# Attention's pooled v taken from a TensorE product of 32-row blocks, with its own loads and GpSimd sums left out, and the merge moved to the head of an iteration

## The chip, the cores and the metric

One core of a Trainium2 chip runs the whole program. The metric is device time in microseconds (us) for one execution; lower is better. Engines are named as in the profile: PE is TensorE (PEld its weight loads), DVE is VectorE, ACT is ScalarE, POOL is GpSimd, SP is the engine that here issues almost all DMAs.

## The reference, cut to what matters

```python
# q, k, v: (4, 8, 576, 64) fp32; factor = 4, Sd = 144
q_d, k_d, v_d = (t.reshape(B, H, Sd, factor, D).mean(axis=3) for t in (q, k, v))
out_up = np.repeat(sm_attn(q_d, k_d, v_d), factor, axis=2)      # pooled attention, 144 x 144
mask = np.abs(pos[:, None] - pos[None, :]) < factor
attn = softmax(np.where(mask, scale * q @ k^T, -1e9))           # local attention, a band of 7
x = (out_up + attn @ v) -> (2304, 512)
x = moe(x)      # two dense layers, 512 -> 2048 -> 512, mish between them
out = moe2(x)   # 8 experts, one chosen per token, 512 -> 1024 -> 512
```

## The kernel before

The program runs in three parts: attention, the dense layers (`moe1`) and the experts (`moe2`). The change touches attention alone.

**Units and iterations.** Attention works on 16 units, one for each batch b (4) and pair of heads (4 in a batch). A loop over `it` = 0..19 (line 561) runs them as a software pipeline, with every engine's instructions in the order in which the code is written: iteration `it` transposes and copies q and k of unit it+1 (`transposes`, L381 to L383 on PE; `copies` and `p_copies`, L392 to L405 on ACT), makes the scores of unit it (`scores`, L413 and L418; `p_scores`, L453), normalizes unit it-1 (`normalize`, L434 to L437; `p_normalize`, L469 to L471), makes the outputs of unit it-2 (`outputs`, L499 for the pooled part, L504 for the local part) and adds both parts up for unit it-3 (`merge`, L518 on DVE, and a store to `x_t` by SP, L533). After the outputs come the softmaxes of unit it (L426 to L428, L462, L464), and `scatter` (L443, L360, L447), `p_transposes` (L479) and `pt_copies` (L486) of unit it-1.

**v stands twice in SBUF.** The local part multiplies by 32-row blocks of v: `load_v(b, n)` issues six DMAs (L340), each with 32 rows of all 8 heads, 64 KB in pieces of 256 bytes; 24 of them fill one of the two tiles `vw` for a batch. One quarter n of a batch is loaded at the end of each iteration. A block starts 4 rows ahead of the 24 rows of queries that it serves, so that 8 rows of each block stand in a neighbour too. The pooled part has loads of its own: `load_v4(j, c)` fetches 288 rows of four heads (288 KB, in pieces of 1 KB, L330), and `pool_v(j, c)` sums groups of four rows in two additions on POOL (L354, L355), once in each iteration, behind `pool_qk` (L347, L348) on the same engine.

**Weights.** `prep_step` spreads the splitting of the dense layers' weights over the iterations (lines L199 to L219 on ACT and DVE, loads L184 and L186 on SP). From iteration 5 on there is some in each iteration.

**PSUM.** Eight banks go around: `bank()` gives the next one at each call, ten calls in an iteration, and whoever writes first into a bank waits for the last reader of its former content. The two banks of the local outputs are read last by `merge`, one iteration later.

**Queues.** All loads and stores of this stage go through SP in the order of the code, so a load that waits for its buffer holds everything written behind it.

Of the kernel before, what the change touches and what calls it, by code (L numbers as in the profile page):

```python
# [23 lines left out]
def moe_kernel(ctx: ExitStack, tc: tile.TileContext, q, k, v, w_in, w_out, modality, w_gate, w_gate_t, m_bias, w1, w2, out):  # L24
# [133 lines left out]
    LAG = 5  # L158
    LA = 1
    SC_A = (0, 1)  # L160
# [80 lines left out]
    NP = H // 2  # L241
# [5 lines left out]
    SPL = S // 4  # L247
    HS = SPL // 2
    CT = S // 128
# [4 lines left out]
    def attention(acx, xcx, tcx):  # L254
# [19 lines left out]
        pbd = [spare[2 + i][:, :2 * S].rearrange("p (t h i q) -> p t h i q", t=T, h=2, i=4) for i in range(2)]  # L274
        vw = [ac.tile([128, T, H * D], F32, name=f"vw{i}") for i in range(2)]
        x0 = ac.tile([128, NP, BT], F32, name="x0")

        def setup_a():
# [26 lines left out]
        def setup_p():  # L305
            for t in pbd:
                G.memset(t, 0.0)
# [18 lines left out]

        def load_v4(j, c):
            b, h0 = j // 2, j % 2 * HB
            v4 = ld.tile([HS, HB, 4, D], F32, tag="v4", name="v4")
            SP.dma_start(out=v4.rearrange("p h r d -> p h (r d)"), in_=v[b, h0:h0 + HB, c * 4 * HS:(c + 1) * 4 * HS, :].rearrange("h (p r) d -> p h (r d)", r=4))  # L330
            bt[j]["v4", c] = v4

        def load_v(b, n):
# [16 lines left out]

        def pool_v(j, c):
            v4 = bt[j]["v4", c]
            vp = wk.tile([HS, HB, D], F32, tag="vp", name="vp", bufs=6)
            G.tensor_tensor(v4[:, :, 0:2], v4[:, :, 0:2], v4[:, :, 2:4], op=ALU.add)  # L354
            G.tensor_tensor(vp, v4[:, :, 0], v4[:, :, 1], op=ALU.add)  # L355
            bt[j]["vp", c] = vp

# [98 lines left out]
        def p_softmax(u):  # L456
            psc = st.pop(("ps", u))
            pe = wk.tile([128, LQ, SPL], F32, tag="pe", name="pe")
            pm = wk.tile([128, LQ], F32, tag="pm", name="pm")
            pz = wk.tile([128, LQ], F32, tag="pz", name="pz")  # L460
            p3 = psc[:, :LQ * SPL].rearrange("p (g s) -> p g s", g=LQ)
            V.tensor_reduce(pm, p3, axis=X, op=ALU.max, negate=True)  # L462
            for g in range(LQ):
                A.activation(pe[:, g], p3[:, g], AF.Exp, bias=pm[:, g:g + 1], accum_out=pz[:, g:g + 1])  # L464
            st["p", u] = (pe, pz)

        def p_normalize(u):
            pe, pz = st["p", u]
            V.tensor_scalar(pz, pz, 1e-9, 4.0, op0=ALU.add, op1=ALU.mult)  # L469
            V.reciprocal(pz, pz)  # L470
            G.tensor_tensor(pe, pe, pz.unsqueeze(2).to_broadcast([128, LQ, SPL]), op=ALU.mult)  # L471

        def p_transposes(u):
            pe, _ = st.pop(("p", u))
            tps = [bank(f"tp{c}") for c in range(2)]
            for c in range(2):
                for g in range(LQ):
                    n = min(128, 2 * SPL - 128 * g)
                    PE.transpose(tps[c][:HS, 128 * g:128 * g + n], pe[:n, g, HS * c:HS * c + HS], ident[:n, :n])  # L479
            st["q", u] = tps  # L480

        def pt_copies(u):
            tps = st[("q", u)]
            pp = wk.tile([HS, 2, 2 * SPL], F32, tag="pp", name="pp", bufs=1)
            for c in range(2):
                A.copy(pp[:, c], tps[c][:HS, :2 * SPL])  # L486
            st["q", u] = pp

        def outputs(u):
            j, p = divmod(u, NP // 2)  # L490
            b, pg = divmod(u, NP)
            vp, w_ = [bt[j]["vp", c] for c in range(2)], vw[b % 2]
            pp = st.pop(("q", u))
# [3 lines left out]
            for c in range(2):  # L497
                for h in range(2):
                    PE.matmul(po[64 * h:64 * h + 64], vp[c][:, 2 * p + h], pp[:, c, SPL * h:SPL * h + SPL], start=c == 0, stop=c == 1, tile_position=(0, 64 * h))  # L499
            o = [bank(f"xo{i}") for i in range(2)]  # L500
# [46 lines left out]
        load_a(1)  # L547
        for c in range(2):
            load_v4(0, c)
        for n in range(NP - 1):  # L550
            load_v(0, n)
            if n == LA:
                load_a(2)
        setup_p()
        for z in range(2):
            pool_qk(1, z, V if z else G)
        pool_v(0, 0)
        load_v4(1, 0)
        copies(0)
        p_copies(0)  # L560
        for it in range(U + 4):
            if it == U - 1:
# [4 lines left out]
                split_x(0, *range(KD))  # L567
            new, mid, old = it < U, 0 < it <= U, 2 <= it < U + 2
            if it + 1 < U:
                transposes(it + 1)  # L570
                copies(it + 1)
                p_copies(it + 1)
            if mid:
                normalize(it - 1)
                p_normalize(it - 1)
            if 3 <= it < U + 3:
                merge(it - 3)
            if new:
# [632 lines left out]
```

## Time and profile before

| what | us |
|---|---|
| median of 3 runs (843.55 to 846.75) | 845.87 |
| the profiled execution's own time | 849.41 |
| its span, first to last instruction | 847.7 |
| PE, DVE, ACT, POOL busy in the span | 761.4, 593.6, 526.9, 220.3 |

The page gives busy time of each engine, a picture of the span in 40 slices (about 21.2 us each), the chain of waits that ended last, and groups of instructions by line. Attention takes about the first eight slices. A row of the timeline has the start, the duration, the engine, the source line, the operation with what it writes and reads, the count, and in square brackets how long the engine sat idle before and who released it. SPq stands for the issue of a DMA by SP's queue. The mean granted TensorE clock over the span is 0.954 of full speed.

### The profile page before, as it was taken

What the parts mean: (1) busy time and instruction counts of PE and PEld (TensorE: products, weight loads), DVE (VectorE), ACT (ScalarE), POOL (GpSimd) and SP (SyncE); (2) the same over time, 40 slices, a digit from 0 to 9 for tenths busy, and PEclk for the clock granted to TensorE, in tenths of its full rate; (3) what the DMA queues carried; (4) which work ended last, traced back from release to release, by engine and by line L of the source; (5) the groups of instructions that cost most, each with busy time, mean ns of one, the idle gap of its engine ahead of it and who ended that gap; (6) DMA issues with size and microseconds to landing.
All of it is one profiled execution on the core that took longest, in us unless ns stands there. A gap on an engine that the chain in (4) does not pass through costs nothing. (4 is left out here: it accounts for less than half of the span.)

```text
span 847.7 us, 14454 instructions
## 1 busy us (share of the span) xinstructions
PE 761.4 (90%) x5078; PEld 644.4 (76%) x5078; DVE 593.6 (70%) x1414; ACT 526.9 (62%) x1019; POOL 220.3 (26%) x212
## 2 busy tenths in 40 slices
PE   5597786799979999999999899899789999999991
PEld 4475665588858888888899788789688887899981
DVE  6499998689966874388439658968766555666652
ACT  6597886899846556655666567554336554565551
POOL 7577673100000000000000110337323232332330
PEclk9699988999979999999999999999999999999996
DMA  7999991455623110010001004546577667767762
GB/s 171 221 185 217 233 239 62 142 149 180 192 66 127 63 26 0 14 57 20 0 13 58 20 29 183 76 39 197 103 223 222 208 194 235 223 228 240 199 213 63
DMA packets 90066, 112.99 MB, mean 133 GB/s; under 512 B 39915, under 2 KB 62077, under 8 KB 89725
## 3 DMA queue, kind: packets, MB, share of 16 engines
q1 hardware_dynamic: 85421, 101.35, 44.7%
q0 software_dynamic: 4560, 10.60, 3.6%
q8 instruction: 42, 0.69, 0.4%
q14 instruction: 43, 0.35, 0.2%
HBM read 97.06 MB, written 15.12 MB: 132 GB/s over the span
## 5 line engine op out<-in xcount | busy, mean ns | idle before, releaser
L731 DVE TENSOR_TENSOR t<-bk,t 128x512 f32<-128x512 f32 (+1 forms) x80 | 50.0, 633 | 100.8 <-ACT t L725 100.8
L678 POOL DMA_INDIRECT ids_by_expert<-tok_id,g_pi x18 | 20.8, 1154 | 279.1 <-DVE run L677 104.3
L638 DVE SCALAR_TENSOR_TENSOR junk<-o,wgb 128x512 f32<-128x512 f32 x120 | 85.0, 708 | 2.9
L719 ACT ACTIVATE t<-bk 128x512 f32<-128x512 f32 (+1 forms) x80 | 44.0, 550 | 54.5 <-PE bk L711 52.8
L740 DVE TENSOR_TENSOR gg<-t,gg 128x512 fp32r<-128x512 f32 (+1 forms) x80 | 57.3, 720 | 7.5 <-ACT gg L729 4.2
L729 ACT CAST gg<-t 128x512 fp32r<-128x512 f32 (+1 forms) x57 | 32.7, 573 | 40.0 <-DVE t L731 33.7
L711 PE MATMUL bk<-x,wi0h 128*128 128x512 f32 (+1 forms) x160 | 52.3, 407 | 5.4 <-DVE x L699 5.1
L720 ACT ACTIVATE t<-t,half 128x512 f32<-128x512 f32 (+1 forms) x80 | 54.6, 682 | 2.6
L1097 POOL DMA_INDIRECT out_dram<-yo,oid x19 | 25.4, 1338 | 115.7 <-ACT yo L1096 69.2
L1083 ACT ACTIVATE hT<-bk 128x256 fp32r<-128x256 f32 x80 | 30.4, 383 | 35.6 <-PE bk L1081 33.1
L725 ACT ACTIVATE t<-t,hpi 128x512 f32<-128x512 f32 (+1 forms) x80 | 52.2, 674 | 0.2
L711 PE MATMUL bk<-x,wi1h 128*128 128x512 f32 (+1 forms) x160 | 47.8, 381 | 4.2 <-DVE t L731 4.2
L751 PE MATMUL bk<-wo1h,gg 128*128 128x512 f32 x144 | 48.3, 406 | 0.0
L1084 DVE SCALAR_TENSOR_TENSOR hT<-bk,hT 128x256 fp32r<-128x256 f32 x80 | 32.9, 420 | 21.5 <-ACT hT L1083 21.4
L711 PE MATMUL bk<-x,wi3h 128*128 128x512 f32 (+1 forms) x160 | 46.9, 375 | 0.6 <-DVE rank L673 0.6
L711 PE MATMUL bk<-x,wi2h 128*128 128x512 f32 (+1 forms) x160 | 46.1, 369 | 0.0
L751 PE MATMUL bk<-wo3h,gg 128*128 128x512 f32 x144 | 46.1, 392 | 0.0
L751 PE MATMUL bk<-wo0h,gg 128*128 128x512 f32 x144 | 45.9, 393 | 0.0
L751 PE MATMUL bk<-wo2h,gg 128*128 128x512 f32 x144 | 45.8, 392 | 0.0
L711 PEld LDWEIGHTS bk<-x,wi0h 128*128 128x128 f32 x160 | 31.9, 204 | 13.6 <-DVE x L699 7.0
L711 PEld LDWEIGHTS bk<-x,wi1h 128*128 128x128 f32 x160 | 30.6, 195 | 8.9 <-DVE t L731 4.6
L1081 PE MATMUL bk<-x,ew10h 128*128 128x256 f32 x160 | 31.8, 288 | 5.7 <-DVE x L1016 2.4
(308 smaller groups left out, 2338.2 us busy)
## 6 DMA issues: line engine op xcount, KB each, us to landing
est<-in_moe_w_dram SPq DMA_DIRECT2D x88, 512.0 KB
wst<-in_moe_w_in_dram SPq DMA_DIRECT2D x16, 512.0 KB
wst<-in_moe_w_out_dram SPq DMA_DIRECT2D x16, 512.0 KB
vw<-in_v_dram SPq DMA_DIRECT2D x88, 64.0 KB
v<-in_v_dram SPq DMA_DIRECT2D x16, 288.0 KB
x_second<-o SPq DMA_DIRECT2D x18, 256.0 KB
kn<-in_k_dram SPq DMA_DIRECT2D x8, 512.0 KB
qn<-in_q_dram SPq DMA_DIRECT2D x8, 512.0 KB
```

Source lines behind the costliest of these rows:

```text
L638: V.scalar_tensor_tensor(wgb["junk"], x2[tl], 1.0, wgb[e], op0=ALU.mult, op1=ALU.mult, accum_out=gate[tl][:, e:e + 1])
L711: PE.matmul(h, a[:, f % QF, kk], x[:, c], start=n == 0, stop=n == 3 * KD - 1)
L719: A.activation(t, bk[f % GF][:, :BLK[j]], AF.Tanh, scale=0.5)
L720: A.activation(t, t, AF.Arctan, scale=-0.5, bias=half)
L725: A.activation(t, t, AF.Sin, scale=-2.0, bias=hpi)
L729: A.copy(gg[:, 0], t_)
L731: V.tensor_tensor(t, bk[f % GF][:, :BLK[j]], t, op=ALU.mult)
L740: V.tensor_tensor(gg[:, 1], t, gg[:, 0], op=ALU.subtract)
L751: PE.matmul(acc[t], gg[:, a, c], w[:, f % QF], start=f == 0 and n == 0, stop=f == NF - 1 and n == 2)
L1081: PE.matmul(ps[:, :256], W1(i, a, kk, f), xt[i][:, c, kk], start=n == 0, stop=n == 3 * KD - 1)
L1083: A.activation(hT[:, 0, f], ps[:, :256], AF.Relu)
L1084: V.scalar_tensor_tensor(hT[:, 1, f], ps[:, :256], 0.0, hT[:, 0, f], op0=ALU.max, op1=ALU.subtract)
```

## The change

- `load_v4` and `pool_v` go, with their 16 loads and 32 POOL additions.
- A constant `pool_v` tile (128 x 32) is made once: column a has ones on the four rows of each block that form pooled row a, 6 columns for each of the 24-row stretches, and zeros in the last 8 columns.
- `pool_vw(b)`, once in a batch at the end of iteration 4b+1, multiplies `pool_v` by the six 512-column tiles of `vw`: six fp32 matmuls into 32-partition strips of two banks, then two copies on ACT into `vp`. Pooled rows so stand at 24 of every 32 partitions, and the pooled probabilities `pe` are laid out the same way: they go to two fixed tiles that POOL clears once, ACT's exponentials and POOL's normalization write 24 of every 32 columns, and `p_transposes`, `pt_copies` and the pooled products work on 128 and 64 rows where they worked on 72 and 72.
- The blocks of batch 0 are all loaded ahead of the loop, before `load_a(2)`; those of batch b+1 at iterations 4b+1 (two quarters), 4b+2 and 4b+3, not one quarter at 4b+1 to 4b+4.
- `merge(it - 3)` stands at the head of an iteration, ahead of the transposes and of `normalize`.

```diff
+        pool_v = ac.tile([128, W], F32, name="pool_v")
+        pes = [ac.tile([128, LQ, T, W], F32, name=f"pe{i}") for i in range(2)]
...
-        def load_v4(j, c):
...
-        def pool_v(j, c):
-            v4 = bt[j]["v4", c]
-            vp = wk.tile([HS, HB, D], F32, tag="vp", name="vp", bufs=6)
-            G.tensor_tensor(v4[:, :, 0:2], v4[:, :, 0:2], v4[:, :, 2:4], op=ALU.add)
-            G.tensor_tensor(vp, v4[:, :, 0], v4[:, :, 1], op=ALU.add)
-            bt[j]["vp", c] = vp
+        def pool_vw(b):
+
+            ps = [bank(f"pv{c}") for c in range(2)]
+            for t in range(T):
+                c, i = divmod(t, 4)
+                PE.matmul(ps[c][32 * i:32 * i + 32], pool_v, vw[b % 2][:, t], tile_position=(0, 32 * i))
+            vp = wk.tile([128, 2, H * D], F32, tag="vp", name="vp", bufs=1)
+            for c in range(2):
+                A.copy(vp[:KP[c], c], ps[c][:KP[c]])
+            st["v"] = vp
...
-                A.activation(pe[:, g], p3[:, g], AF.Exp, bias=pm[:, g:g + 1], accum_out=pz[:, g:g + 1])
+                A.activation(pe[:, g, :, :QB], p3[:, g].rearrange("p (t a) -> p t a", t=T), AF.Exp, bias=pm[:, g:g + 1], accum_out=pz[:, g:g + 1])
...
-        for c in range(2):
-            load_v4(0, c)
-        for n in range(NP - 1):
+        for n in range(NP):
             load_v(0, n)
-            if n == LA:
-                load_a(2)
+        load_a(2)
...
+            if 3 <= it < U + 3:
+                merge(it - 3)
             if it + 1 < U:
                 transposes(it + 1)
...
-            if 3 <= it < U + 3:
-                merge(it - 3)
...
-            m, odd = divmod(it + 1, 2)
-            b, n = divmod(it + NP - 1, NP)
-            if b < B:
-                load_v(b, n)
-            if m < NH:
-                pool_v(m, odd)
-            if m + 1 < NH:
-                load_v4(m + 1, odd)
+            b, n = divmod(it, NP)
+            if n == 1 and b < B:
+                pool_vw(b)
+            if n and b + 1 < B:
+                for z in ((), (0, 1), (2,), (3,))[n]:
+                    load_v(b + 1, z)
```

Line numbers of the changed kernel are 5 or 6 higher in the functions below `pool_vw`: L479 becomes L485, L381 becomes L386, L518 becomes L524.

The first place is PE at the end of iteration 1. The rows are PE's instructions from the pooled scores of unit 1 to the first transposes of unit 3; `bk` is a PSUM bank, `rl` the relaid k or q. Before:

```order
L453 MATMUL bk_95<-kp,qbd_168 128x144 x3
L479 MATMUL bk_96<-ident,pe 72x128 x2
L479 MATMUL bk_96<-ident,pe 72x32
L479 MATMUL bk_97<-ident,pe 72x128 x2
L479 MATMUL bk_97<-ident,pe 72x32
L381 MATMUL bk_90<-ident,rl 128x128 x4
L382 MATMUL bk_92<-ident,pl 128x128
```

and now:

```order
L458 MATMUL bk_95<-kp,qbd_168 128x144 x3
L485 MATMUL bk_96<-ident,pe_172 128x128 x2
L485 MATMUL bk_96<-ident,pe_172 128x32
L485 MATMUL bk_97<-ident,pe_172 64x128 x2
L485 MATMUL bk_97<-ident,pe_172 64x32
L357 MATMUL bk_90<-vw_169,pool_v 32x512 x4
L357 MATMUL bk_91<-vw_169,pool_v 32x512 x2
L386 MATMUL bk_92<-ident,rl 128x128 x4
L387 MATMUL bk_94<-ident,pl 128x128
```

Six products with 512 columns that read all of `vw` now stand ahead of the transposes of unit 3, and the banks that follow are two further on.

The second place is SP's queue from the loads ahead of the loop to the end of iteration 1 or 2. Before:

```order
L330 DMA v_267<-in_v_dram 72x4x256
L330 DMA v_269<-in_v_dram 72x4x256
L340 DMA vw_169<-in_v_dram 28x8x64
L340 DMA vw_169<-in_v_dram 32x8x64 x11
L323 DMA kn<-in_k_dram 128x4x256
L324 DMA rm<-in_k_dram 64x4x64
L323 DMA qn<-in_q_dram 128x4x256
L324 DMA rm<-in_q_dram 64x4x64
L340 DMA vw_169<-in_v_dram 32x8x64 x6
L330 DMA v_309<-in_v_dram 72x4x256
L184 DMA wst<-in_moe_w_in_dram 128x4x128
L340 DMA vw_169<-in_v_dram 32x8x64 x5
```

and now:

```order
L341 DMA vw_169<-in_v_dram 28x8x64
L341 DMA vw_169<-in_v_dram 32x8x64 x22
L341 DMA vw_169<-in_v_dram 28x8x64
L330 DMA kn<-in_k_dram 128x4x256
L331 DMA rm<-in_k_dram 64x4x64
L330 DMA qn<-in_q_dram 128x4x256
L331 DMA rm<-in_q_dram 64x4x64
L183 DMA wst<-in_moe_w_in_dram 128x4x128
```

All 24 blocks of batch 0 stand in one run ahead of the third pair of k and q loads; before, that pair and a weight load stood between them.

The third place is DVE from the scatter of one unit to the next softmax, in an iteration of batch 1 where no weights are split. Before:

```order
L443 STREAM_TRANSPOSE et<-e 128x384
L360 TENSOR_REDUCE spare_101<-et 32x12x24 x2
L434 TENSOR_REDUCE sm<-e 128x12
L435 TENSOR_SCALAR sm<-sm 128x12
L436 RECIPROCAL sm<-sm 128x12
L469 TENSOR_SCALAR pz<-pz 128x3
L470 RECIPROCAL pz<-pz 128x3
L518 TENSOR_TENSOR x_171<-bk_92,pos 128x288
L518 TENSOR_TENSOR x_171<-bk_93,pos 128x224
L518 TENSOR_TENSOR x<-bk_93,pos 128x64
L360 TENSOR_REDUCE rl<-qn 128x512
```

and now:

```order
L448 STREAM_TRANSPOSE et<-e 128x384
L365 TENSOR_REDUCE spare_101<-et 32x12x24 x2
L524 TENSOR_TENSOR x_174<-bk_94,pos 128x288
L524 TENSOR_TENSOR x_174<-bk_95,pos 128x224
L524 TENSOR_TENSOR x<-bk_95,pos 128x64
L439 TENSOR_REDUCE sm<-e 128x12
L440 TENSOR_SCALAR sm<-sm 128x12
L441 RECIPROCAL sm<-sm 128x12
L474 TENSOR_SCALAR pz<-pz 128x3
L475 RECIPROCAL pz<-pz 128x3
L365 TENSOR_REDUCE rl<-qn 128x512
```

The three additions of the merge stand ahead of the normalization; nothing else on DVE has moved there.

## Rows read from the trace of the kernel before

**Rows 1.** Busy time by stretch; columns: us, then busy us of each engine
```profile
core 0: us, PE busy (x) PEld busy (x) DVE busy (x) ACT busy (x) POOL busy (x), PEclk, DMA share, GB/s
24.00:41.40 17.40, 9.26 (x108) 6.79 (x106) 7.82 (x22) 8.83 (x27) 10.46 (x12) 0.65 1.12 230
41.40:60.80 19.40, 18.86 (x316) 15.16 (x315) 16.45 (x39) 18.63 (x65) 13.93 (x15) 0.97 0.88 176
60.80:134.00 73.20, 60.45 (x935) 47.34 (x934) 70.07 (x138) 61.58 (x198) 51.98 (x52) 0.91 0.95 221
...
250.00:600.00 350.00, 340.67 (x1659) 290.75 (x1658) 237.98 (x682) 207.38 (x325) 52.30 (x34) 0.99 0.24 63
```
**Rows 2.** Timeline of PE and POOL, 24 to 42 us
```profile
24.07 0.33 PE L413 MATMUL bk<-mask,id_b 128*128 128x384 bf16 x1
...
31.07 0.59 PE L504 MATMUL bk<-spare,vw 128*64 128x96 f32 x4 [3.79 <-DMA vw<-in_v_dram]
31.92 1.26 POOL L354 TENSOR_TENSOR v<-v 72x512 f32<-72x512 f32 x1 [4.53 <-DMA v<-in_v_dram]
...
36.60 0.59 PE L504 MATMUL bk<-spare,vw 128*64 128x96 f32 x4 [0.93 <-DMA vw<-in_v_dram]
...
41.37 0.53 PE L413 MATMUL bk<-mask,id_b 128*128 128x384 bf16 x1
```
**Rows 3.** Timeline of SP's DMA issues, 0 to 40 us
```profile
6.61 1.88 SPq L330 DMA_DIRECT2D v<-in_v_dram  x2
8.60 12.19 SPq L340 DMA_DIRECT2D vw<-in_v_dram  x12
20.89 0.40 SPq L323 DMA_DIRECT2D kn<-in_k_dram  x1
...
23.35 3.06 SPq L340 DMA_DIRECT2D vw<-in_v_dram  x6
...
28.46 3.86 SPq L340 DMA_DIRECT2D vw<-in_v_dram  x6
```
**Rows 4.** Timeline around iteration 6, 63 to 71 us
```profile
63.20 0.35 SPq L533 DMA_DIRECT2D x_t<-x  x1
...
66.43 0.43 PE L504 MATMUL bk<-spare,vw 128*64 128x96 f32 x4 [2.05 <-DMA vw<-in_v_dram]
...
68.83 0.82 DVE L518 TENSOR_TENSOR x<-bk,pos 128x288 f32<-128x288 f32 x2 [1.11 <-DMA x_t<-x]
```
**Rows 5.** Groups of DVE instructions by line, 60.8 to 134 us; count, busy us, mean ns
```profile
L204 DVE TENSOR_SCALAR wm<-wm 128x512 int32<-128x512 int32 x5 | 8.8, 1754 | 0.0
...
L214 DVE SCALAR_TENSOR_TENSOR wm<-wst,wm 128x512 int32<-128x512 int32 x5 | 5.7, 1135 | 0.0
...
L219 DVE TENSOR_TENSOR wi0l<-wm,wi0h 128x512 fp32r<-128x512 f32 x3 | 4.1, 1360 | 0.0
L209 DVE SCALAR_TENSOR_TENSOR wm<-wst,wm 128x512 int32<-128x512 int32 x4 | 4.1, 1016 | 0.0
L469 DVE TENSOR_SCALAR pz<-pz 128x3 f32<-128x3 f32 x9 | 3.2, 355 | 0.0
```
**Rows 6.** The same lines by source, whole span: ns least/median/most
```profile
L204 DVE TENSOR_SCALAR wm<-wm x32: 417/428/3674, 70.2 to 236.4; 128x512 int32<-128x512 int32 x32
L469 DVE TENSOR_SCALAR pz<-pz x16: 103/105/1412, 18.9 to 149.6; 128x3 f32<-128x3 f32 x16
L209 DVE SCALAR_TENSOR_TENSOR wm<-wst,wm x32: 681/692/1762, 88.8 to 243.1; 128x512 int32<-128x512 int32 x32
```
**Rows 7.** Groups of POOL instructions by line, 60.8 to 134 us
```profile
L354 POOL TENSOR_TENSOR v<-v 72x512 f32<-72x512 f32 x10 | 13.6, 1358 | 9.3 <-DMA v<-in_v_dram 9.1
...
L355 POOL TENSOR_TENSOR vp<-v 72x256 f32<-72x256 f32 x10 | 7.3, 731 | 0.8
```
**Rows 8.** Timeline of PE, 76 to 84 us: tiled fp32 matmuls
```profile
78.00 0.88 PE L418 MATMUL bk<-spare,qT 128*32 128x64 f32 x48
81.73 1.16 PE L504 MATMUL bk<-spare,vw 128*64 128x96 f32 x24
```
**Rows 9.** Groups by line, 0 to 170 us: a full-width ACT copy; POOL memset
```profile
L394 ACT COPY qT<-bk 128x512 f32<-128x512 f32 x16 | 9.4, 587 | 0.2
...
L307 POOL MEMSET spare<- 128x1152 f32 x2 | 2.3, 1166 | 0.1
```
**Rows 10.** Timeline around iteration 15, 138 to 145 us
```profile
141.96 0.23 DVE L436 RECIPROCAL sm<-sm 128x12 f32<-128x12 f32 x1
142.33 0.81 DVE L518 TENSOR_TENSOR x<-bk,pos 128x288 f32<-128x288 f32 x2
...
142.84 1.23 PE L504 MATMUL bk<-spare,vw 128*64 128x96 f32 x12 [4.83 <-DVE x L518]
```

More of the change, by code (lines that the diff above doesn't have):

```diff
@@ L158, in moe_kernel @@
     LAG = 5
-    LA = 1
     SC_A = (0, 1)
@@ L247, in moe_kernel @@
     SPL = S // 4
-    HS = SPL // 2
+    KP = (128, 32 * (T - 4))
     CT = S // 128
@@ L285, in setup_a @@
             V.tensor_copy(pool_id[:, :, RP:], ident[:2 * CR, :2 * CR].rearrange("p (z r) -> p z r", z=2))
+            V.memset(pool_v, 0.0)
+            V.tensor_reduce(
+                pool_v[:, :QB].rearrange("p (i a) -> p i a", i=4),
+                ident.rearrange("p (i w) -> p i w", i=4)[:, :, 4:4 + QB].rearrange("p i (a f) -> p i a f", f=4),
+                axis=X, op=ALU.add,
+            )
             V.tensor_copy(id_b, ident)
@@ L305, in setup_p @@
         def setup_p():
-            for t in pbd:
+            for t in pbd + pes:
                 G.memset(t, 0.0)
@@ L325, in load_a @@
             bt[j] = {"n": (kn, qn), "rm": rm}
-        def load_v4(j, c):
[L328 to L331, printed above, removed]
         def load_v(b, n):
@@ L457, in p_softmax @@
             psc = st.pop(("ps", u))
-            pe = wk.tile([128, LQ, SPL], F32, tag="pe", name="pe")
+            pe = pes[u % 2]
             pm = wk.tile([128, LQ], F32, tag="pm", name="pm")
@@ L470, in p_normalize @@
             V.reciprocal(pz, pz)
-            G.tensor_tensor(pe, pe, pz.unsqueeze(2).to_broadcast([128, LQ, SPL]), op=ALU.mult)
+            p4 = pe[:, :, :, :QB]
+            G.tensor_tensor(p4, p4, pz.unsqueeze(2).unsqueeze(3).to_broadcast([128, LQ, T, QB]), op=ALU.mult)
         def p_transposes(u):
@@ L478, in p_transposes @@
                     n = min(128, 2 * SPL - 128 * g)
-                    PE.transpose(tps[c][:HS, 128 * g:128 * g + n], pe[:n, g, HS * c:HS * c + HS], ident[:n, :n])
+                    PE.transpose(tps[c][:KP[c], 128 * g:128 * g + n], pe[:n, g, 4 * c:min(4 * c + 4, T)].rearrange("p t a -> p (t a)"), ident[:n, :n])
             st["q", u] = tps
@@ L483, in pt_copies @@
             tps = st[("q", u)]
-            pp = wk.tile([HS, 2, 2 * SPL], F32, tag="pp", name="pp", bufs=1)
+            pp = wk.tile([128, 2, 2 * SPL], F32, tag="pp", name="pp", bufs=1)
             for c in range(2):
-                A.copy(pp[:, c], tps[c][:HS, :2 * SPL])
+                A.copy(pp[:KP[c], c], tps[c][:KP[c], :2 * SPL])
             st["q", u] = pp
@@ L491, in outputs @@
             b, pg = divmod(u, NP)
-            vp, w_ = [bt[j]["vp", c] for c in range(2)], vw[b % 2]
+            vp, w_ = st["v"], vw[b % 2]
             pp = st.pop(("q", u))
@@ L498, in outputs @@
                 for h in range(2):
-                    PE.matmul(po[64 * h:64 * h + 64], vp[c][:, 2 * p + h], pp[:, c, SPL * h:SPL * h + SPL], start=c == 0, stop=c == 1, tile_position=(0, 64 * h))
+                    PE.matmul(po[64 * h:64 * h + 64], vp[:KP[c], c, (2 * pg + h) * D:(2 * pg + h + 1) * D], pp[:KP[c], c, SPL * h:SPL * h + SPL], start=c == 0, stop=c == 1, tile_position=(0, 64 * h))
             o = [bank(f"xo{i}") for i in range(2)]
@@ L556, in attention @@
             pool_qk(1, z, V if z else G)
-        pool_v(0, 0)
-        load_v4(1, 0)
         copies(0)
```

## The prediction

> **What bounds the kernel now.** I read the busy time by stretch first, with the starts of iterations as bounds, then the timeline in the stretch that looked worst, then the groups by line where an engine was full. The reader is to see four stages in [rows 1]. From 24 to 41 us nothing is full: one iteration takes 17.3 us, the TensorE clock is 0.65, and the DMA engines are the busy ones. From 41 to 61 us iterations take about 6.5 us, and ACT (18.63 of 19.40) and PE (18.86) are full. From 61 to 134 us nine iterations take 8.1 us each, and DVE is full (70.07 of 73.20). Behind attention PE is full (340.67 of 350.00 in the long middle); nothing there changes, so what attention gains or loses shifts the end by as much.
>
> The slow iteration has its reason in the timeline: the local outputs of unit 0 wait for blocks of v, 3.79 us in the first of three such waits, and end at 37.2; POOL sits 4.53 us for v rows meanwhile [rows 2]. SP shows why: the first 12 blocks took 12.19 us to issue, the third k and q load stands before the next six, and the last six go out at 28.46 to 32.3 [rows 3]. The same wait, shorter, comes in iteration 6 (2.05 us), where DVE also waits 1.11 us for an earlier store [rows 4].
>
> In the DVE stage the full engine isn't only at work. L204 takes 417 ns at best and up to 3674; five of them here mean 1754 [rows 5, 6]. Whenever I looked, POOL was inside an addition at that time. Above their least times (L214 and L219 have about L209's least time, 0.68 us) the groups of [rows 5] carry: L204 5 x 1.34 = 6.7, L214 5 x 0.455 = 2.3, L219 3 x 0.68 = 2.0, L209 4 x 0.335 = 1.3, L469 9 x 0.252 = 2.3 us; 14.6 us together, a fifth of the stage.
>
> **The change part by part.**
>
> *The start: -4.0 us.* The wait for batch 0's blocks moves from the outputs in iteration 2 to the pooled product at the end of iteration 1, where PE's queue is held with the transposes of unit 3 behind it. When are 24 blocks there? SP is free for them at about 8.5 us. The first eight I leave at the old pace of 1.02 us (they came behind two v loads that are gone, so this is slow enough: 16 us); the other 16 at 0.51 to 0.64 us (3.06 and 3.86 for six, [rows 3]) make 24 to 26 us, landing some 2 us later. With about 1 us for the last pair of products PE goes on at 27 to 29 us. Then come the transposes, scores and outputs of iteration 2, 6 to 8 us by the clock, so that iteration 3's transposes start at 33 to 37 us, where they started at 38.65, behind the last wait of [rows 2]. The middle is a gain near 4 us. Bounds: -7 (blocks at 0.51 us from the first) and +4 (all 24 at 1.02 us: 33 us, and outputs at about 41). The k and q loads of unit pair 2 are issued 3 to 5 us later than at 20.89; they are first needed in iteration 2, which starts later too.
>
> *Iteration 6: -1.5 us.* Batch 1's last blocks are issued an iteration earlier, so the 2.05 us wait goes; DVE's next limit is close (its own 1.11 us, [rows 4]), so I take 1.5, between 0 and 2.
>
> *POOL's additions: -5.0 us.* In the DVE stage they are 13.6 + 7.3 = 20.9 of POOL's 51.98 us [rows 1, 7], 40%. In proportion, 14.6 x 0.40 = 5.9 us of DVE's excess go. I take 5.0, because the merge no longer stands between the normalization and the weight splitting, which so falls nearer to the start of POOL's remaining run of additions. Bounds: nothing (the rest of POOL's work meets DVE as before) and 9.3 us (if the excess falls as the square of what is left, 0.6). In other stages ACT, PE or DMA set the pace, and I count nothing there.
>
> *The pooled products: +2.1 us.* No row has an fp32 product with 512 columns in strips of 32. The nearest: 24 products of 64 columns, four strips wide, take 0.88 us, so 6 streams of 64 columns, 2.3 ns a column; 12 products of 96 columns, two wide, take 1.16, so 2.0 ns a column [rows 8]. A batch has a stream of four and one of two, 1024 columns: 2.1 to 2.4 us side by side; one after the other, six times 512 columns at 2.0 ns, 6.2 us. I take 2.1. The Trainium skill ("TensorE: Matmul & The Clock Gate", "Why this matters for your kernels") has three strips of 32 with 512 columns gain 2.38 times, not 3; by that I would estimate 2.6 us and the sum would be 0.5 us higher; the four-wide row stands between. Iteration 1 has its product inside the first term. Iteration 5 lies where PE and ACT are full, so it pays in full; the two copies on ACT, 2 x 0.587 us [rows 9], run while PE does the next transposes. Iterations 9 and 13 lie in the DVE stage, where PE and ACT have some 12 us to spare in nine iterations [rows 1]: nothing. If DVE's excess fell so far that PE became the bound, they would cost up to 2 us each.
>
> *The merge ahead of the normalization: -1.0 us.* DVE does as much as before. At iteration 15 the second half of the outputs waits 4.83 us for the merge, which stands behind normalization steps from 141.16 to 142.33 us [rows 10]; it comes 1.2 us earlier. I take 1.0; bounds 0 and 1.2. The normalization itself starts 0.81 us later, covered by POOL, which waits for DVE in every iteration.
>
> *SP's new order: +1.0 us.* At iterations 5 and 9, twelve blocks (6 to 10 us by [rows 3]) stand ahead of a store of `x_t`. The tile that the store reads has two buffers, and DVE's merge two iterations on waits for it; the 1.11 us of [rows 4] is that wait, for a store issued 5.6 us earlier. Iterations of 6.5 to 8 us leave 13 to 16 us for load, blocks, store and landing, so it just fits; I take one more wait like the one seen.
>
> *Small ones: +0.8 us.* Transposes and pooled products on 128 rows where there were 72 load wider weights: 0.5 over 16 units (nothing where PE has room). One memset and one reduction more on DVE ahead of the loop: 0.3. Two clears of 128 x 576 on POOL, 0.6 us each by half of L307 [rows 9], take the place of two sums there. The exponentials, copies and normalization have as many elements as before: nothing. The 16 loads taken out lighten DMA queues that are 0.88 to 1.12 busy [rows 1]; what that gives is in the terms above.
>
> Sum: -4.0 - 1.5 - 5.0 + 2.1 - 1.0 + 1.0 + 0.8 = **-7.6 us**. It is made against the profiled execution, 849.41 us, and gives 841.8 there. That execution lies 3.5 us above the median of the runs, 845.87; I carry the difference over: **838.3 us**.
>
> **The rivals.**
>
> *PE held at the start, no gain there (843 us).* A queue that works in order stands still until the last block lands. The old stall dropped the clock to a mean of 0.65 [rows 1]; a new stall of 5 us in iteration 1 can do the same, and iteration 2 then runs at 1.2 GHz. The Trainium skill (same page, same section) warns that an idle gap between bursts of matmuls brings the half clock back; the trace agrees with its 0.65. The first term becomes 0 to +1: 845.9 - 3.1 = 842.8. For it: 12 blocks did take 12.19 us. Against: six took 3.06, with no k or q load between.
>
> *DVE stays slow (843 us).* The excess is made by POOL's remaining 31 us as before, since those run right behind the normalization, where the weight splitting falls. The third term is 0: 843.3. For it: L204's wait is longer than any one addition. Against: the additions removed stand right ahead of L469 of the next iteration, and it is in the list.
>
> *More than forecast (830 us).* DMA is the hidden bound: with 4.7 MB less, blocks land at the fast pace (-7), the merge's wait goes (-1 instead of +1) and DVE's excess falls by 9. That is -7.6 - 3 - 2 - 3 = -15.6, so 830.3. For it: a DMA share near 1 for 120 us. Against: in the DVE stage no engine but POOL waits long for a load.
>
> *Stores behind the blocks (851 us, slower).* If twelve blocks go out at 1.02 us, as the first twelve did, the store issues 12 us into the iteration pair and lands 4 to 5 us after DVE wants it, at iterations 5, 8 and 12: 3 x 4.5 = 13.5 us with DVE full, in place of my 1.0. Then -7.6 + 12.5 = +4.9: 850.8. It decides from about 10 us for twelve blocks on. Against: 0.51 to 0.8 us is the usual pace later on.
>
> **How the numbers follow.** A measurement of this kernel can tell about 0.5% (4.2 us) from no change. Forecast 0.55 and "more" 0.13 are faster; "PE held" 0.14 and "DVE stays" 0.11 fall within 0.5%; the stores 0.07, slower. So 0.68, 0.25 and 0.07. The range reaches from "more" to a start or a DVE stage that gives nothing, with 4 us of the pooled products on top (one after the other): 830 to 847. It leaves out the slow case and the ends of the others, less than 2 in 10.
>
> **What would show it.** Right: the scores of unit 3 near 37 us and not 41.37; the last wait for `vw` on the pooled product and none on L510; L357 about 2 us a batch; L203 and L474 means in the DVE stage down by a third or more; iterations of about 7.5 us there; the middle from 250 on unchanged in length. Wrong: the pooled product of batch 0 ending after 31 us, a wait of DVE's merge for `x_t` over 2 us, L203 still at 1.7 us, or PE full in iterations 9 and 13.

## The result and the profile after

The changed kernel takes 831.64 us (median of 4 runs, 829.33 to 833.56) where the kernel before took 846.31 in the same comparison: ratio 0.985, 95% interval 0.9816 to 0.9884. A second comparison gave 0.9848 (0.9821 to 0.9876; 828.71 against 842.27). The gain of 13.6 to 14.7 us is nearly twice the 7.6 forecast. The profiled execution took 833.11 us, with a span of 831.4.

The busy time of the changed kernel by stretch, bounded by the scores of units 2, 3, 6 and 15 as in [rows 1] (the last line is the long middle, 12 us earlier):

```profile
core 0: us, PE busy (x) PEld busy (x) DVE busy (x) ACT busy (x) POOL busy (x), PEclk, DMA share, GB/s
27.40:34.50 7.10, 6.65 (x107) 4.87 (x105) 4.45 (x11) 5.81 (x20) 5.61 (x6) 1.00 1.11 300
34.50:55.80 21.30, 21.30 (x329) 15.11 (x327) 18.25 (x52) 20.95 (x71) 12.13 (x14) 1.00 0.76 176
55.80:122.20 66.40, 62.41 (x960) 43.29 (x957) 58.55 (x134) 63.26 (x206) 32.52 (x31) 1.00 0.75 188
238.00:588.00 350.00, 341.80 (x1665) 291.44 (x1664) 240.43 (x695) 207.40 (x326) 52.48 (x34) 0.99 0.25 64
```

Three things differ from [rows 1]. The iteration behind unit 2's scores takes 7.1 us and not 17.4, after iteration 1 has become longer (unit 2's scores begin at 27.4 and not 24.0). The nine iterations take 66.4 us and not 73.2, and now ACT (63.26) and PE (62.41) fill them; DVE has fallen from 70.07 to 58.55. And the DMA share, 0.95 there before, is 0.75. The granted clock is 1.00 in all three stretches (0.65, 0.97 and 0.91 before; the two levels are 1.2 and 2.4 GHz).

SP's issues and PE's timeline at the start (the last row of PE is iteration 5):

```profile
7.66 15.23 SPq L341 DMA_DIRECT2D vw<-in_v_dram  x24
22.99 0.39 SPq L330 DMA_DIRECT2D kn<-in_k_dram  x1
...
29.56 13.41 SPq L341 DMA_DIRECT2D vw<-in_v_dram  x18
43.08 0.40 SPq L539 DMA_DIRECT2D x_t<-x  x1
...
58.34 7.64 SPq L341 DMA_DIRECT2D vw<-in_v_dram  x12
66.08 0.40 SPq L539 DMA_DIRECT2D x_t<-x  x1
```

```profile
22.53 1.90 PE L357 MATMUL bk<-vw,pool_v 128*32 128x512 f32 x10
25.04 1.02 PE L357 MATMUL bk<-vw,pool_v 128*32 128x512 f32 x2 [0.61 <-DMA vw<-in_v_dram]
...
29.41 0.86 PE L505 MATMUL bk<-pp,vp 128*64 128x144 f32 x8
30.20 1.21 PE L510 MATMUL bk<-spare,vw 128*64 128x96 f32 x24
...
34.52 0.33 PE L418 MATMUL bk<-mask,id_b 128*128 128x384 bf16 x1
...
52.56 1.91 PE L357 MATMUL bk<-vw,pool_v 128*32 128x512 f32 x12
```

All 24 blocks go out in 15.23 us, 0.63 us each, where the first twelve alone took 12.19 [rows 3]. PE waits 0.61 us for the last of them, and the outputs (L510) wait for nothing; before, they waited three times [rows 2]. DVE's groups in the nine iterations, against [rows 5] (count, busy us, mean ns, idle before):

```profile
L524 DVE TENSOR_TENSOR x<-bk,pos 128x288 f32<-128x288 f32 x16 | 6.6, 453 | 4.6 <-DMA x_t<-x 3.6 <-PE bk L386 0.9
...
L213 DVE SCALAR_TENSOR_TENSOR wm<-wst,wm 128x512 int32<-128x512 int32 x5 | 4.3, 868 | 0.0
L208 DVE SCALAR_TENSOR_TENSOR wm<-wst,wm 128x512 int32<-128x512 int32 x4 | 3.6, 894 | 0.0
L218 DVE TENSOR_TENSOR wi0l<-wm,wi0h 128x512 fp32r<-128x512 f32 x3 | 3.5, 1171 | 0.0
L203 DVE TENSOR_SCALAR wm<-wm 128x512 int32<-128x512 int32 x5 | 3.2, 631 | 0.0
...
L474 DVE TENSOR_SCALAR pz<-pz 128x3 f32<-128x3 f32 x8 | 0.8, 105 | 0.0
```

L203 (L204 before) has a mean of 631 ns and not 1754, L474 (L469) 105 and not 355. Below, DVE's "excess" is counted over all its operations between the scores of units 6 and 15: duration less the least of the same line and shape, where that is over 60 ns. It was 15.5 us before and is 4.5 now.

**Where the time went.** The scores of unit 3 begin 6.9 us earlier, those of unit 6 5.0, of unit 15 11.8, the first matmul of layer 1 14.8 (129.2 and not 144.0). Layer 2 begins 11.9 us earlier, since the stretch between takes 40.0 us and not 37.1; the dense layers end 14.1 us earlier.

### The profile page after: what moved, and what is told of

The parts are those of the page before. It is cut to its first block, busy times and chain, and to the rows that moved or that the text cites. A ratio compares the mean times of both kernels' runs of the same rounds, so it can differ in the third digit from the quotient of the medians.

```text
span 831.4 us, 14515 instructions
## 1 busy us (share of the span) xinstructions
PE 765.1 (92%) x5126; PEld 637.0 (77%) x5126; DVE 581.5 (70%) x1416; ACT 529.1 (64%) x1027; POOL 192.7 (23%) x182
## 3 DMA queue, kind: packets, MB, share of 16 engines
q1 hardware_dynamic: 80621, 96.63, 42.7%
## 5 line engine op out<-in xcount | busy, mean ns | idle before, releaser
L710 PE MATMUL bk<-x,wi0h 128*128 128x512 f32 (+1 forms) x160 | 50.4, 394 | 5.5 <-DVE x L698 5.1
L992 POOL DMA_INDIRECT xg<-x_second,tid x22 | 25.2, 1147 | 43.1 <-DMA tid<-ids_by_expert,ridx 20.9
```

Source lines behind the costliest of these rows:

```text
L710: PE.matmul(h, a[:, f % QF, kk], x[:, c], start=n == 0, stop=n == 3 * KD - 1)
L992: G.indirect_dma_start(out=xg[i][z], out_offset=None, in_=x2d, in_offset=bass.IndirectOffsetOnAxis(ap=tid[i][z], axis=0), bounds_check=NT ...
```

## The experiments

All were run against the kernel before, with a ratio each. Behind attention a profile says little: the changed kernel profiled a second time agreed with the first to 0.2 us at unit 15, at layer 1 and at the end of the dense layers, and yet its span was 826.3 us and not 831.4, all of it from the experts. So attention is read from the marks, and the time from the ratio. The marks scatter too: e5 and e6 differ from the changed kernel and from e4 only by a third tile for x, which is of no use before iteration 5, and their unit 3 begins 1.5 and 1.7 us earlier already.

| kernel | unit 3 | unit 6 | unit 15 | layer 1 | DVE excess | time to before (95%) |
|---|---|---|---|---|---|---|
| before | 41.4 | 60.8 | 134.0 | 144.0 | 15.5 | 1 |
| changed | 34.5 | 55.8 | 122.2 | 129.2 | 4.5 | 0.985 (0.9816 to 0.9884) |
| e12, changed again | 34.5 | 55.8 | 122.4 | 129.0 | 4.5 | 0.9848 (0.9821 to 0.9876) |
| e1, changed + POOL additions | 35.4 | 56.9 | 122.0 | 129.0 | 5.6 | 0.9865 (0.9834 to 0.9895) |
| e2, before + blocks first | 42.7 | 62.1 | 134.2 | 144.2 | 14.2 | 1.0005 (0.9983 to 1.0026) |
| e4, changed + v rows | 38.5 | 65.9 | 142.2 | 149.3 | 4.5 | 1.005 (1.0027 to 1.0072) |
| e6, e4 + three x tiles | 36.8 | 66.6 | 135.8 | 143.3 | 4.7 | 1.0031 (1.0 to 1.0063) |
| e9, changed + thin v rows | 34.2 | 58.6 | 125.6 | 132.6 | 4.5 | 0.9918 (0.9877 to 0.996) |
| e7, before + merge first | 39.5 | 58.7 | 129.6 | 138.0 | 8.8 | 0.9956 (0.9926 to 0.9987) |
| e8, changed, merge behind | 34.3 | 56.1 | 123.6 | 132.0 | 5.0 | 0.9877 (0.9827 to 0.9927) |
| e5, changed + three x tiles | 33.0 | 55.1 | 118.5 | 125.6 | 4.5 | 0.9822 (0.9775 to 0.9869) |
| e10, e5 + scatter on POOL | 35.0 | 56.2 | 126.7 | 133.0 | 8.3 | 0.9848 (0.9803 to 0.9892) |
| e11, changed, blocks even | 33.5 | 56.8 | 122.5 | 129.5 | 4.5 | 0.9813 (0.9779 to 0.9847) |

(Starts of scores and of layer 1's first matmul, and DVE's excess, in us.)

**e1: POOL's additions back, on a tile of zeros.**

```diff
+                G.tensor_tensor(dum[:, :, 0:2], dum[:, :, 0:2], dum[:, :, 2:4], op=ALU.add)
+                G.tensor_tensor(dum[:, :, 3], dum[:, :, 0], dum[:, :, 1], op=ALU.add)
```

> The changed kernel with two additions per iteration put back on POOL at their old place, in the old shapes (72 x 512 and 72 x 256), on a tile of zeros that nobody else reads and no DMA fills; the output is unchanged. Theory (the additions themselves slowed DVE): from unit 6 to unit 15 DVE's time above its operations' least times rises from 4.5 us to 9 to 14 us, L203 (here one or a few lines further down) from 631 ns to over 1.1 us in the mean, the nine iterations from 66.4 to 70 to 73 us, and the kernel takes 831.6 + 5 = 836.6 us (834.5 to 839.5). Rival (the v rows' traffic, or the merge's new place, made DVE faster): the nine iterations stay within 1 us of 66.4 and the time within 1.5 us of 831.6. Second rival (ACT and PE are the bound now, so a slower DVE is partly hidden): DVE's excess rises as in the theory, but the time by under 2 us.

The theory fell, and the first rival's time came (831.35; its nine iterations, 65.1 us, are even 1.3 shorter than 66.4). POOL is as busy as before and DVE hardly notices (the stretch, then two groups of POOL and one of DVE):

```profile
56.90:122.00 65.10, 61.62 (x959) 43.37 (x957) 59.64 (x134) 63.02 (x205) 51.14 (x49) 1.00 0.76 189
```

```profile
L609 POOL TENSOR_TENSOR dum<-dum 72x512 f32<-72x512 f32 x9 | 11.6, 1289 | 0.0
...
L610 POOL TENSOR_TENSOR dum<-dum 72x256 f32<-72x256 f32 x9 | 7.2, 805 | 0.7
```

```profile
L203 DVE TENSOR_SCALAR wm<-wm 128x512 int32<-128x512 int32 x5 | 3.2, 633 | 0.0
```

POOL's 51.14 us of 65.10 answer to 51.98 of 73.20 in [rows 1]; layer 1 begins at 129.0.

**e2: the order of the blocks alone, on the kernel before.**

```diff
-        for n in range(NP - 1):
+        for n in range(NP):
             load_v(0, n)
-            if n == LA:
-                load_a(2)
+        load_a(2)
```

(and the quarter that iteration 0 loaded is left out there)

> The kernel before, with all 24 blocks of batch 0 issued ahead of the third k and q load (the last six were issued in iteration 0, behind it); v rows, POOL's sums and everything else as they were. Theory (the order of the blocks on SP is what held the start): scores of unit 3 begin near 37 us where they began at 41.4, and the time falls by 3 to 6 us, to 842 (840.3 to 843.3). Rival (the v rows' loads, which go ahead of the blocks, and POOL's wait for them held the start as well): scores of unit 3 begin at 39.5 or later, and the time falls by less than 2 us from 846.3.

The rival. The outputs' waits for blocks are gone, and unit 3's scores begin no earlier (42.7), since everything behind the blocks on SP came later. The waits from 24 to 40 us (us in all, times, longest):

```profile
PE bk L479 <- POOL pe L471: 10.5, 1, 10.5
POOL h L347 <- DMA kn<-in_k_dram: 8.9, 1, 8.9
DVE rl L360 <- DMA qn<-in_q_dram: 8.0, 1, 8.0
...
POOL v L354 <- DMA v<-in_v_dram: 2.2, 1, 2.2
```

POOL waits for k rows, then for v rows, and PE waits 10.5 us for the normalization that stands behind both on POOL.

**e3: the merge behind the normalizations, first attempt.**

```diff
-            if 3 <= it < U + 3:
-                merge(it - 3)
...
                 p_normalize(it - 1)
+            if 3 <= it < U + 3:
+                merge(it - 3)
```

> The changed kernel with the merge put back behind both normalizations, where it stood before. Theory (as forecast, the merge's place is worth 1 us, at the end of attention): the second half of the outputs at iteration 15 and the first matmul of layer 1 start about 1 us or more later (130.2 or later, where it was 129.2), and the time rises by 1.0, to 832.6. Rival A (the wait at iteration 15 only moves, since layer 1 waits for weights or for x later on): the first matmul moves, the time stays within 0.7 of 831.6. Rival B (the place of the merge took POOL's normalization out of DVE's weight splitting): DVE's time above least times from unit 6 to 15 rises from 4.5 to over 7 us and the time rises by 2.5 us or more.

It gives a reason for moving the merge, read from the code: a pooled product takes two banks more, the ring of eight comes round sooner, and a merge at the old place adds up a bank that the transposes have filled. So x is another one, the part behind the dense layers takes 358.3 us and not 265.7, and the 938.82 us say nothing of the merge. e8 repeats it with the ring left as it was.

**e4: the 16 loads of v rows back, read by nobody.**

```diff
+            v4 = ld.tile([72, HB, 4, D], F32, tag="v4", name="v4")
+            SP.dma_start(out=v4.rearrange("p h r d -> p h (r d)"), in_=v[b, h0:h0 + HB, c * 288:(c + 1) * 288, :].rearrange("h (p r) d -> p h (r d)", r=4))
```

> The changed kernel with the 16 loads of whole rows of v (4.7 MB) put back at their old places on SP; nobody reads what they bring, and the output is unchanged. Theory (traffic costs where DMA is the bound only, at the start): the blocks go out some 2 us later behind two v loads, the first pooled product ends near 28 us where it ended at 26.1, scores of unit 3 begin 2 us after 34.5, the nine iterations from unit 6 to 15 stay within 1 us of 66.4, and the time rises by 2, to 833.6 (832.5 to 835.5). Rival (DMA is the hidden bound through the whole of attention): the nine iterations take 69 us or more and the time rises by 4 us or more. If the time does not rise by 1 us, the traffic was worth nothing and the gain is all in the order and in POOL.

The rival, and more: the time is above that of the kernel before. The stretches, the waits from 14 to 150 us, and two rows of SP:

```profile
38.50:65.90 27.40, 23.69 (x330) 16.34 (x327) 17.18 (x47) 21.57 (x71) 11.00 (x12) 0.88 0.90 188
65.90:142.20 76.30, 65.23 (x959) 45.40 (x957) 60.49 (x140) 64.15 (x206) 33.65 (x32) 0.96 0.84 202
```

```profile
DVE x L529 <- DMA x_t<-x: 16.6, 6, 6.9
POOL h L353 <- DMA kn<-in_k_dram: 9.8, 1, 9.8
DVE rl L370 <- DMA qn<-in_q_dram: 8.5, 1, 8.5
```

```profile
8.85 17.94 SPq L341 DMA_DIRECT2D vw<-in_v_dram  x24
...
35.88 10.68 SPq L341 DMA_DIRECT2D vw<-in_v_dram  x12
```

Behind two loads of v rows the 24 blocks of batch 0 take 17.94 us to issue and not 15.23. The next twelve take 10.68, but so they do without the rows (10.5 for the first twelve of the 18 that the changed kernel issues from 29.56 us on); what differs is that they start 6.3 us later and that v loads stand behind them, and so the first store of `x_t` goes out at 51.42 us and not at 43.08. DVE's excess stays at 4.5: the loads slow no operation of DVE, they make engines wait.

**e6: e4 with three tiles for x.**

```diff
-            x = wk.tile([128, S], F32, tag="x", name="x")
+            x = wk.tile([128, S], F32, tag="x", name="x", bufs=3)
```

> The kernel of the run that loads the rows of v for nobody (847.4 us; unit 6 to unit 15 in 76.3 us, where the changed kernel takes 66.4), with three buffers for the merged tile. It tells how the loads cost their 16 us: DVE waited 16.6 us in six waits for stores of x_t that stood on SP behind blocks and v rows. Theory (the order on SP: a store late behind loads): the waits fall below 4 us, iteration 5 gets back under 10 us (it took 14.3), unit 6 to 15 falls to 68 to 70 us, and the time to 836 to 840. Rival (DMA bandwidth: 4.7 MB at some 200 GB/s are 24 us, wherever the wait shows): the waits for stores turn into waits for vw, kn or qn, unit 6 to 15 stays above 73 us and the time above 843.

Neither quite. DVE's waits for the stores fall to 1.4 us, and layer 1 comes 6.0 us earlier (1.7 of it stand at unit 3 already); iteration 5 takes 16.8 us, since the waits are now for loads:

```profile
POOL h L353 <- DMA kn<-in_k_dram: 18.2, 4, 8.9
PE bk L362 <- DMA vw<-in_v_dram: 9.6, 3, 5.8
DVE rl L370 <- DMA qn<-in_q_dram: 9.5, 2, 6.9
```

Against the kernel with three tiles and no v rows (e5), unit 15 is 17.3 us late. The nine iterations (69.2) met the theory's number, the time of 843.72 the rival's.

**e9: the same loads with a sixteenth of the bytes.**

```diff
-            ... out=v4.rearrange("p h r d -> p h (r d)"), in_=v[...]
+            ... out=v4[:, :, 0, :D // 4], in_=v[...][:, :, :D // 4]
```

> The changed kernel with the 16 extra loads again at their places on SP, for nobody, but a sixteenth of the bytes: 288 packets each as before, of 64 bytes and not of 1024 (0.29 MB in all, where it was 4.7). It tells what the rows of v cost by: bytes on the DMA engines, or 16 more issues on SP and a queue whose order they change. Theory (bytes): blocks of batch 0 out by 24 us, scores of unit 3 begin within 1.5 us of 34.5, unit 6 to 15 within 2.5 us of 66.4, time 833 (831 to 836). Rival (issues and order on SP): nearly as slow as with the whole rows, 843 or more, with DVE waiting over 10 us for stores of x_t.

The theory: the blocks of batch 0 are out at 22.8 us,

```profile
7.88 14.89 SPq L341 DMA_DIRECT2D vw<-in_v_dram  x24
```

the nine iterations take 66.9 us, layer 1 begins at 132.6, and the time is 834.63. As many issues and packets cost 3.4 us at layer 1, nearly all of it in iteration 5 (11.4 us and not 8.2); the bytes of e4 make up the other 16.7.

**e7 and e8: the merge's place, on either kernel.** e7 moves it to the head in the kernel before; e8 moves it back in the changed kernel, with the product's banks taken without moving the ring:

```diff
             st["v"] = vp
+            turn[0] -= 2
```

> The kernel before with the merge at the head of the iteration, as in the changed kernel; all else, the v rows and POOL's sums of them too, as before. It asks what took DVE's stretched operations away, now that POOL's additions alone do not bring them back (the run with additions on a tile of zeros: DVE's excess over least times 5.6 us, against 4.5 without and 15.5 in the kernel before). Theory (the merge's place: DVE's weight splitting no longer falls into POOL's run of additions): DVE's excess from unit 6 to 15 falls from 15.5 to under 8 us, the nine iterations from 73.2 to 69 or less, the time by 3 to 5 us, to 840 (838.5 to 842). Rival (POOL's waits for v rows, 20 us in eight waits, push its additions and normalizations into DVE's splitting): excess stays above 11 us and the time within 1.5 us of before.

> The changed kernel with the merge back behind the normalizations, and the two PSUM banks of a pooled product taken from those that the next transposes use, without moving the ring of eight on (with ten banks an iteration and two more in every fourth, a merge at the old place would read banks that the transposes have filled again; that is what made the attempt before this one compute another x). Theory as forecast: the merge's place is worth 1 us at the end of attention and nothing elsewhere: 832.6 (831 to 834). Rival (the merge's place is what freed DVE): excess from unit 6 to 15 rises from 4.5 to over 9 us, the nine iterations from 66.4 to 69 or more and the time to over 835. Second rival (the head is the worse place, because there DVE waits for stores of x_t with the normalization queued behind): the waits fall, and the time falls by 1 to 3 us.

In the kernel before the place is worth 6.0 us at layer 1, and DVE's excess falls from 15.5 to 8.8. L204's mean, 1754 ns in [rows 5], is there

```profile
L204 DVE TENSOR_SCALAR wm<-wm 128x512 int32<-128x512 int32 x5 | 4.2, 832 | 0.0
```

The excess lies between the theory's bound and the rival's, the time (839.02) where the theory had it; the nine iterations (70.9 us) missed the theory's 69. In the changed kernel (e8) the place is worth 2.8 us at layer 1, 0.5 us of excess, and nothing that the time can tell (0.9877 against 0.985; 832.88 us, in the theory's range). Its waits for `x_t` fall from 4.3 to 0.2 us, the second rival's sign, but the time doesn't fall.

So DVE was slowed by the way in which additions, late v rows and the late merge fell together: 15.5 us of excess with all three, 8.8 with the merge first (e7), then 5.6 without the rows (e1) or 4.5 without the additions (e4), and 5.0 with the late merge alone (e8). Additions or rows alone with the late merge were not run. The traces tell which operations met. The first L204 of the nine iterations, in the kernel before:

```profile
69.94 0.72 POOL L355 TENSOR_TENSOR vp<-v 72x256 f32<-72x256 f32 x1
70.16 3.67 DVE L204 TENSOR_SCALAR wm<-wm 128x512 int32<-128x512 int32 x1
...
70.63 0.83 POOL L437 TENSOR_TENSOR e<-e,sm 128x384 f32<-128x384 f32 x1
71.42 0.90 POOL L471 TENSOR_TENSOR pe<-pe,pz 128x432 f32<-128x432 f32 x1
...
72.28 1.27 POOL L347 TENSOR_TENSOR h<-kn 128x512 f32<-128x512 f32 x1
...
73.63 0.80 POOL L348 TENSOR_TENSOR pl<-h 128x256 f32<-128x256 f32 x1
```

and the same instruction in e7:

```profile
68.49 0.53 DVE L204 TENSOR_SCALAR wm<-wm 128x512 int32<-128x512 int32 x1
```

In the kernel before it lasts through five instructions of POOL in a row. Of the 15.5 us, 8.0 stand in operations that overlap an addition of v, and 7.6 in others that overlap the pooling of k or q (L347, L348). With the merge first (e7) 5.0 and 2.2 are left, with 1.6 over normalizations alone. So the late merge put DVE's splitting into the pooling of k and q as well, and not only into the additions.

**e5: three tiles for x in the changed kernel.**

> The changed kernel with three buffers for the merged tile that the store of x_t reads, in place of two. Theory (DVE's 4.3 us of waits for that store, four of them, are in the way, since the merge now heads the iteration): no wait of L524 for x_t, the stretch from unit 5's scores on gets 2 to 4 us shorter, time 831.6 - 2 = 829.6 (828 to 830.6). Rival (ACT, busy 63 of 66 us, and PE, 62 of 66, are the bound from unit 6 to 15): the waits go, and the time stays within 1 us of 831.6.

(The edit is that of e6.) The waits for `x_t` go, 4.3 us in four, as the theory had it. Attention gets 3.6 us shorter, 1.5 of them ahead of unit 3, where the third tile is of no use yet, and 2.1 behind it. The time (827.08) is below the theory's range, but by the ratio it can't be told from the changed kernel. The stretch:

```profile
55.10:118.50 63.40, 60.95 (x960) 43.39 (x957) 58.52 (x134) 62.13 (x204) 30.96 (x30) 1.00 0.81 199
```

**e10: one scatter copy on POOL.**

```diff
-                (A.copy if i in SC_A else copy_1)(pb[r, :, i], et[r, :, :QB])
+                (A.copy if i in SC_A[:1] else G.tensor_copy if i in SC_A else copy_1)(pb[r, :, i], et[r, :, :QB])
```

> The kernel with three buffers for the merged tile (827.1 us), with one of ACT's two scatter copies an iteration (32 x 288, 0.42 us each) moved to POOL, which is idle for half of the stretch. Theory (ACT, busy 62.45 of 63.5 us from unit 6 to 15, is what sets the pace now): iterations get 0.2 to 0.4 us shorter, attention 3 to 5 us, time 823.5 (822 to 825.5). Rival A (PE, 61.05 of 63.5, is the bound as well): under 1.5 us of gain, 826 or more. Rival B (POOL's queue: the copy waits for DVE's transpose with the pooling of k and q behind it, and the outputs wait for the copy): POOL waits for et, the outputs for POOL, and the time rises to 829 or more.

Rival B, with another wait than it named. ACT falls to 59.87 us in the nine iterations, which take 70.5, and POOL stands in its queue (waits from 14 to 140 us):

```profile
POOL spare L452 <- PE bk L510: 18.1, 8, 4.0
...
POOL spare L452 <- DVE et L448: 13.2, 6, 3.3
```

The outputs (L510) wait for no copy of POOL's; PE waits 2.2 us for the pooled k and q, which stand behind the copy (not at all in e5), and the rest of the loss is not told apart. Layer 1 comes 7.3 us later than in e5 (5.4 of it behind unit 3), DVE's excess is 8.3, and the time is 829.94.

**e11: the blocks a quarter an iteration.**

```diff
-            if n and b + 1 < B:
-                for z in ((), (0, 1), (2,), (3,))[n]:
-                    load_v(b + 1, z)
+            b, n = divmod(it + NP - 1, NP)
+            if it and b < B:
+                load_v(b, n)
```

> The changed kernel with the blocks of later batches issued a quarter an iteration, as before the change (six each in four iterations and not 12, 6, 6 in three; the last six end one iteration later, just ahead of the pooled product that needs them). Theory (as forecast: 1.5 us gained in iteration 6 by earlier blocks, 1.0 lost to stores of x_t behind twelve blocks): DVE's waits for x_t fall from 4.3 to under 2 us, PE waits 1 to 3 us for vw in iterations 5, 9 and 13, and the time is 831.6 + 0.5 (830.5 to 833.5). Rival A (twelve blocks in a row are the worse price): the waits for x_t go, none for vw comes, and the time falls by 2 to 4 us. Rival B (the product's need of all 24 blocks at one point is the worse price): PE waits over 4 us for vw at each product and the time rises by 3 us or more.

In the trace mostly the theory: no wait for `x_t`, one wait of PE for `vw` (1.3 us, in iteration 9), iteration 5 at 10.2 us and not 8.2, layer 1 at 129.5. The time reads 827.82, where Rival A had it, so it was asked whether the changed kernel itself reads lower:

> The changed kernel itself once more, as a yardstick: its own time rests on four runs (831.6 us, ratio to before 0.985, interval 0.9816 to 0.9884), and the runs with three buffers for the merged tile (0.9822) and with the blocks spread evenly (0.9813) lie only 2 to 3 us below it by ratio. If those two are real gains, the ratio comes out at 0.985 or above again. If they are the scatter of the measurement, it comes out near 0.982, as they did, and of the two only what the trace shows is left: layer 1 begins 3.6 us earlier with three buffers (125.6 against 129.2), and no earlier with the even blocks (129.5).

It stayed at 0.9848, so the yardstick had not read high; but its interval overlaps those of e5 and e11, and neither is shown to be faster than the changed kernel. By the trace e5 is the better version, by 2.1 us from unit 3 to layer 1, and e11 is not.

## Why the prediction was right, and where it failed

**Right:** the sign, the range, and most of what was to be seen: scores of unit 3 ahead of 37 us, waits on the pooled product only, L203 and L474 down by far more than a third, 7.4 us an iteration. **Wrong:** the size, and the reason given for two terms; and one of its own signs of being wrong came, PE full in iterations 9 and 13.

- *The step that failed* is "The 16 loads taken out lighten DMA queues that are 0.88 to 1.12 busy [rows 1]; what that gives is in the terms above". It had no term of its own, and it is the largest part: of the parts that were put back one at a time, only the rows cost more than 3 us. e4 puts 4.7 MB back and loses 20.1 us at layer 1, two per cent of the time (17.7 with three tiles for x, e6 against e5); e9 shows that it is the bytes. That is their price in the changed order. No run takes the rows out of the kernel before, so the 14.8 us at layer 1 can't be shared out by adding: e7 alone had 6.0 of them. The trace of before had the price:

```profile
14.00:122.00 108.00, 84.78 (x1259) 66.46 (x1263) 92.14 (x193) 87.97 (x289) 74.35 (x77) 0.87 0.97 209
```

4.7 MB at 209 GB/s, with a DMA share of 0.97, is 22.5 us (an estimate). The rival "More than forecast" named DMA as the hidden bound and gave 830; it was argued down with "no engine but POOL waits long for a load", and POOL's waits were the sign. Of its three parts the fast blocks came, and an excess down by more than its 9 us, though e7 puts most of that on the merge; the merge's wait did not go. Its sum is off by 1 us: 9 less the forecast's 5 is 4 and not 3, so 829.

- *The start, -4.0:* 6.9 came. The mechanism was half right. The order alone gives nothing (e2); with v rows but without POOL's sums of them unit 3 begins at 38.5 and 36.8 (e4 and e6, which have the other parts of the change too), without the rows at 34.5. The bound at the fast pace, -7, was the right end.
- *Iteration 6, -1.5:* 3.2 (6.55 us and not 9.72); the block wait and DVE's own wait for `x_t` went together.
- *POOL's additions, -5.0:* the excess fell by 11.0, so the amount was there, but e1 gives the additions' share as 1.1 without the rows, and e7 gives the merge's place 6.7. The additions meet DVE less when POOL doesn't wait for v rows and the merge stands first. The iterations got only 6.8 us shorter; ACT (63.26 of 66.40) and PE (62.41) then fill them.
- *Pooled products, +2.1:* 1.91 us for batches 1 and 3 (2.98 for batch 2, with a wait of 0.84 for a weight load in it), and iteration 5 takes 1.9 us more than before. The Trainium skill ("TensorE: Matmul & The Clock Gate", "Why this matters for your kernels") gave an estimate of 2.6, and [rows 8] gave 2.1 to 2.4; the trace decides, below both. But in iterations 9 and 13 they are not free: the case in which PE becomes the bound came true.

```profile
76.02:85.39 9.37, 9.37 (x119) 5.30 (x117) 8.38 (x19) 9.06 (x28) 4.29 (x4) 1.00 1.02 244
108.67:117.23 8.56, 8.44 (x119) 5.26 (x117) 8.32 (x19) 8.44 (x28) 2.14 (x2) 1.00 0.62 195
```

Most others take 6.5 to 7.1 us. Iteration 12 takes 9.3 too, without a product; there PE waits 1.7 us for ACT and DVE 1.6 for `x_t`.

- *The merge, -1.0:* 6.0 at layer 1 in the kernel before (e7), where it frees DVE, which the forecast counted only as a reason to take 5.0 for the additions; 2.8 in the changed kernel (e8), gone by the time layer 2 begins, though the dense layers end 2.3 us apart.
- *SP's order, +1.0:* 4.3 us of waits, worth 2.1 us from unit 3 to layer 1 (e5). This term was too small.
- *Small ones, +0.8:* no run measures them apart, but the 0.5 for wider products was too small. From the pooled products' start to the local ones it is 0.79 us in a unit and was 0.54, which is 4 us over 16 units, and PE had little room any more. PE's busy time in an iteration without a product of blocks rose from 6.11 us (before) to 6.55:

```profile
54.51:60.85 6.34, 6.11 (x108) 4.92 (x105) 6.12 (x16) 6.23 (x23) 5.07 (x6) 1.00 0.91 167
55.82:62.37 6.55, 6.55 (x107) 4.87 (x105) 5.11 (x14) 6.41 (x22) 2.80 (x4) 1.00 0.70 174
```

- *"Stores behind the blocks"* is what e4 shows: six waits for `x_t`, 16.6 us. The changed kernel with the rows in loses to the old one (1.005); it didn't come to that because the bytes went at the same time.

## What to carry to other kernels

Where the DMA share is near 1, price the bytes by themselves: bytes taken out over the measured rate, whatever engine shows the wait. Here that gives 22.5 us where the runs show 17 to 20; it is one case. A wait on a full resource moves when the order changes (from blocks to k rows in e2, from stores to k, q and v in e6) and goes only when the load does. An engine that is long idle for loads counts as a waiting engine even if it is not the bound, when another engine's work stands behind those loads in its queue.

## What the runs showed of the hardware

How busy POOL is doesn't tell how much it slows DVE: 51 to 52 us of work went with 15.5 us of excess in the kernel before and with 5.6 in e1. The Trainium skill ("SBUF — State Buffer", "SBUF: two separate sides") says that DVE and GpSimd share a pair of ports as an exclusive lock for a whole instruction, for DVE instructions in a two-port mode or with two inputs in SBUF. The numbers fit that, since then it counts which instructions meet; no run shows the lock itself. The issue of 24 blocks of 64 KB on SP at the start takes 15.23 us in the changed kernel, 14.89 behind two thin loads (e9) and 17.94 behind two whole ones (e4), for the same instructions; why is not shown. And two profiles of the changed kernel agree to 0.2 us at unit 15, at layer 1 and at the end of the dense layers (565.7 us), and then the experts differ by 5 us.
